# Attention block with a gated feed-forward, one Trainium2 core: start-up loads, a bias transposed on TensorE, and the last tile stored in three parts

## The chip, the cores and the metric

The kernel runs on one NeuronCore of one Trainium2 chip. The metric is device time in microseconds (us) of one execution, the median over several executions. TensorE is called PE here, VectorE DVE, ScalarE ACT, GpSimd POOL and SyncE SP. "PEld" is the weight load of a matmul, which the profile lists apart from the matmul.

## The reference

The block normalises x (2048 rows of 512), feeds the result to attention over a cached K and V (32 heads of 128, 2048 keys) and to a feed-forward layer of width 1792 with squared ReLU, and adds the product of both to x:

```python
def _A_ref(x, k_cache, v_cache, wq, wo):
    q = (x @ wq).reshape(B, Sq, 32, 128).transpose(0, 2, 1, 3)
    scores = jnp.einsum("bhqd,bhkd->bhqk", q, k_cache) * (128 ** -0.5)
    p = _softmax(scores, axis=-1)
    o = jnp.einsum("bhqk,bhkd->bhqd", p, v_cache)
    return o.transpose(0, 2, 1, 3).reshape(B, Sq, 32 * 128) @ wo

def _B_ref(x, w1, b1, w2, b2):
    h = jnp.einsum("bsd,df->bsf", x, w1) + b1
    r = jnp.where(h > 0, h, 0)
    return jnp.einsum("bsf,fd->bsd", r * r, w2) + b2

xn = _layernorm(x)
return x + _A_ref(xn, ...) * _silu(_B_ref(xn, ...))
```

All inputs are bf16.

## The kernel before

**Groups and steps.** The 2048 query rows are cut into four blocks of 512. A group `g` is one head of one block, so there are 128 groups. Each group is cut into eight steps `k`, and each step takes two tiles of 128 keys; the steps of the whole kernel are counted by `pi`, from 0 to 1023. A step issues two score matmuls (128x512, `psA<-qt_sb,kT`), one exponential on ACT over both (`pT<-psA`, 128x1024), and, for the step two back, eight matmuls of the probabilities with V (`psO<-v_sb,pT`, 128x129; column 129 is the sum of the row). The eight PV matmuls go to two PSUM banks of `psO`, two query tiles each. After the last step of a group, DVE copies the two banks out (`o_un<-psO`), takes the reciprocal of the sums and writes the normalised tile `o_bf`; a DMA transposes that to `oT`.

**Fillers.** All other matmuls are cut into single 128x512 matmuls and are put between the scores and the PV matmuls of a step, mostly one or two in each: the query projection of later groups (`job_proj`, `psF<-xnT,wq_sb`), the first feed-forward layer (`job_h`), the second (`job_o2`) and the output projection (`job_wo`). `fill_one` takes them from a list sorted by due time; a credit spreads what is left evenly over the steps. The jobs use the two PSUM banks of `psF` in turn, so that a job's first matmul waits until DVE has emptied the bank used two jobs earlier. Each engine runs its instructions in the order in which they are emitted.

**Order of the PV matmuls.** `gen_pv` goes through a step's matmuls key tile by key tile (n = 0, 1), all four query tiles in each; only the last step of a group (k = 7) goes bank by bank. The first PV step of a group (k = 0) waits for the copies of the group before: its matmuls 1 and 2 need the first bank, matmul 3 the second.

**Start.** The DMAs of the start are emitted in a fixed order. SP issues x tile 0, K of group 0, V of group 0, the query weights `wq` of groups 1 and 2, chunk 0 of `w1` (`load_w1(0)`), K and V of group 1 and chunks 1 to 3 of `w1`. Only then come the refills that belong to a step: `wq` of group `g+3` and K of group `g+2` in step k = 0, V of group `g+2` in step k = 1. ACT issues x tiles 1 to 3 and `wq` of group 0. DVE, POOL and ACT normalise the four x tiles, PE transposes them, and the first query projection is done in four parts (`first_proj`). DVE empties them in two copies (`first_evac`), after which the first scores can start. PE runs matmuls on a tile of zeros (`warm_up`) ahead of that.

**Bias.** `b1` (1792 values) is needed with 128 consecutive values down the partitions, 14 columns. A DMA issued by POOL gathers it in that layout (`_dma_gather`, L217), and DVE casts it to f32 (`b1f`) directly after the two first copies. `job_h` adds it.

**End.** The output projection of the last 16 heads is written out by hand as a tail. The last query tile is done in two halves of 256 columns; each half ends in two DVE operations (`tmp_t`, then `out_t`) and a store from SP.

Of the kernel before, what the change touches and what calls it, by code (L numbers as in the profile page):

```python
# [5 lines left out]
ACT = mybir.ActivationFunctionType  # L6
ALU = mybir.AluOpType
BF16 = mybir.dt.bfloat16
F32 = mybir.dt.float32
P = 128  # L10
# [201 lines left out]
    return e.dma_start(out, in_, transpose=True)  # L212


def _dma_gather(nc, e, out, in_):
    with nc.allow_non_contiguous_dma(reason="tiny one-time bias gather"):
        return e.dma_start(out, in_)  # L217


def bass_recurrent_scan__mha_block_cached__dense_activation_squared_relu__prompt_kernel(  # L220
    nc: bass.Bass,
    A_x: bass.AP,
# [11 lines left out]
    _, Sq, D = A_x.shape  # L234
# [4 lines left out]
    NQB = Sq // QB  # L239
    TPB = QB // P  # L240
# [3 lines left out]
    NFC = F // P  # L244
# [7 lines left out]
    CH = [[(m * HC, (m + 1) * HC) for m in range(NCH)] for _ in range(NQB - 1)]  # L252
# [4 lines left out]
    S = _Sched()  # L257
    PE = S.eng("PE")
    AC = S.eng("ACT")
    DV = S.eng("DVE")  # L260
    GP = S.eng("POOL")
    SP = S.eng("SP")
    E = S.emit

    sb = nc.alloc_sbuf_tensor
# [12 lines left out]
    qt_sb = sb("qt_sb", [P, NQS, QB], BF16)  # L278
# [4 lines left out]
    r_t = sb("r_t", [P, 2, QB], BF16)  # L283
    z_t = sb("z_t", [P, 2, D], F32)
    th_t = sb("th_t", [P, 2, D], BF16)
    b1b = sb("b1b", [P, NFC], BF16)
    b1f = sb("b1f", [P, NFC], F32)
    b2bc = sb("b2bc", [P, D], BF16)
    x_ln = sb("x_ln", [P, TPB, D], BF16)
# [6 lines left out]
    ident = sb("ident", [P, P], BF16)  # L296
# [11 lines left out]
    def bankF(i):  # L308
        return psF[:, i * 512:(i + 1) * 512]
# [8 lines left out]
    sl_b1 = S.slot("b1")  # L318
# [10 lines left out]
    t_ident = E(GP, partial(_ts, out=ident[:], in0=identf[:], scalar1=0.0, scalar2=None,  # L329
                            op0=ALU.is_equal), deps=[t_idf])  # L330
# [11 lines left out]
    def ln_load(j, i, eng=SP):  # L342
        jt = j * TPB + i
        t_xl[jt] = S.emit_dma(
            eng, partial(_dma, out=x_ln[:, i, :], in_=A_x[0, jt * P:(jt + 1) * P, :]), sl_xl[i],
            deps=[t_xn.get(jt - TPB)])
# [60 lines left out]
                  deps=[t_wqfill[0], tok_xT[0][i]], inc=(c == NDC - 1))  # L407
        t_proj[0] = t

    def first_evac(i, n):  # L410
        t_evac[0] = t_bankF[i // 3] = E(
            DV, partial(_copy, out=qt_sb[:, 0, i * P:(i + n) * P],
                        in_=bankF(i // 3)[:, i * P:(i + n) * P]), deps=[t_proj[0]])

    def warm_up(n):
        for _ in range(n):
# [4 lines left out]
    t_kfill = [None] * NG  # L421
# [4 lines left out]
    t_proj = [None] * NG  # L426
    t_evac = [None] * NG
# [3 lines left out]
    t_exp = [None] * NPAIR  # L431
# [36 lines left out]
    def gen_scores(pi):  # L468
        g, k = divmod(pi, NPR)
        s2, i = pi % 2, g % NSL  # L470
        assert t_kfill[g] is not None and t_evac[g] is not None
        t = None
        for n in range(2):
            tt = 2 * k + n
            t = E(PE, partial(_mm, out=psA[:, s2 * 1024 + n * 512:s2 * 1024 + (n + 1) * 512],
                              lhsT=kT[:, i, tt * P:(tt + 1) * P], rhs=qt_sb[:, g % NQS, :],
                              start=True, stop=True),
                  deps=[t_exp[pi - 2] if pi >= 2 else None, t_kfill[g], t_evac[g]],
                  inc=(n == 1))
        if k == NPR - 1:  # L480
            t_S_last[g] = t
        t_exp[pi] = E(AC, partial(_act, out=pT[:, pi % NPT, :],
                                  in_=psA[:, s2 * 1024:(s2 + 1) * 1024],
                                  func=ACT.Exp, scale=SM_SCALE),
                      deps=[t, t_PV[pi - NPT] if pi >= NPT else None])

    def gen_pv(pi):
        g, k = divmod(pi, NPR)
        i = g % NSL
        last = k == NPR - 1  # L490
        order = [(n, qt) for n in range(2) for qt in range(TPB)]
        if last:
            order = [(n, qt) for b in range(2) for qt in (2 * b, 2 * b + 1) for n in range(2)]
        t_bank = [None, None]
        t = None
        for idx, (n, qt) in enumerate(order):
            tt, b = 2 * k + n, qt // 2
            tt_first = tt == 0
            inc = idx == 7 or (last and idx == 3)
            t = E(PE, partial(_mm_shared, out=psO[:, b, qt % 2, 0:Dh + 1],  # L500
                              lhsT=pT[:, pi % NPT, n * QB + qt * P:n * QB + (qt + 1) * P],
                              rhs=v_sb[:, i, tt, 0:Dh + 1],
                              start=(tt_first and qt % 2 == 0), stop=(tt == NKT - 1)),
                  deps=[t_exp[pi], t_vfill[g], t_ones,
                        t_oev[g - 1][b] if g >= 1 else None], inc=inc)
            if inc:
                t_bank[b] = t
        t_PV[pi] = t
        if last:
            t_PV_last[g] = t  # L510
            s = g % 2
            for b in range(2):
                t_oev[g][b] = E(DV, partial(_copy, out=o_un[:, s, 2 * b:2 * b + 2, 0:Dh + 1],
                                            in_=psO[:, b, :, 0:Dh + 1]),
                                deps=[t_bank[b], t_onorm[g - 2] if g >= 2 else None])
            tr = E(DV, partial(_recip, out=rden[:, s, :], in_=o_un[:, s, :, Dh]),
                   deps=[t_oev[g][0], t_oev[g][1], t_onorm[g - 2] if g >= 2 else None])
            base = rden[:, s, :]
            rb = bass.AP(tensor=base.tensor, offset=base.offset,
                         ap=[list(base.ap[0]), [1, TPB], [0, Dh]])  # L520
            t_onorm[g] = E(DV, partial(_tt, out=o_bf[:, s, :, :], in0=o_un[:, s, :, 0:Dh], in1=rb,
                                       op=ALU.mult),
                           deps=[tr, tok_oT[g - 2] if g >= 2 else None])
# [8 lines left out]
    t_bankF = [None, None]  # L532
# [8 lines left out]
    t_rt = [None, None]  # L541
# [13 lines left out]
    def at(step, fn):  # L555
        events.setdefault(step, []).append(fn)

    def job_proj(g):
# [15 lines left out]
            return t_evac[g]  # L574
        return NDC, mm, evac

    def job_h(j, c):
        js = slice(j * QB, (j + 1) * QB)
        box = [None]

        def mm(n, bank):
            box[0] = E(PE, partial(_mm, out=bankF(bank), lhsT=w1_sb[:, n, c * P:(c + 1) * P],
                                   rhs=xnT[:, n, js], start=(n == 0), stop=(n == NDC - 1)),
                       deps=[tok_w1[w1_chunk(c)], t_bankF[bank]] + tok_xT[j], inc=(n == NDC - 1))

        def evac(bank, step):
            s = c % 2
            t1 = E(DV, partial(_ts, out=r_t[:, s, :], in0=bankF(bank), scalar1=b1f[:, c:c + 1],
                               scalar2=0.0, op0=ALU.add, op1=ALU.max),
                   deps=[box[0], t_b1, t_rt[s]])  # L590
            t_h2[j, c] = t_rt[s] = E(
                DV, partial(_tt, out=h2T[:, c, :], in0=r_t[:, s, :], in1=r_t[:, s, :],
                            op=ALU.mult),
                deps=[t1] + [t_o2[j - 1, qt] for qt in range(TPB) if j > 0])
            return t1
        return NDC, mm, evac
# [101 lines left out]
                                op=ALU.add), deps=[t, tok_xt[jt]])  # L698


    jobs = []
    for g in range(1, NG):
        jobs.append((NPR * g - 15, NPR * (g - 2), job_proj(g), g))
    for j in range(NQB):
        b = 30 + j * (SPB - 6)
        for c in range(NFC):
            k = b + (SPB * 9 // 256) * c
            jobs.append((k, max(k - 130, 4), job_h(j, c), None))
        for qt in range(TPB):
            k = b + (SPB * 9 // 256) * NFC + (SPB * 28 // 256) * qt  # L710
# [32 lines left out]

    m, half = len(CH[-1]) - 1, D // 2
    nt = H - CH[-1][-1][0]
    tail = [job_wo(NQB - 1, m, qt) for qt in range(TPB - 1)]
    tail.append(job_wo(NQB - 1, m, TPB - 1, 0, half))
    tail.append(job_wo(NQB - 1, m, TPB - 1, half, D))  # L750
    n_in, n_after = 14, 22
    n2 = n_in + n_after - 2 * (nt - 1)
    tail_order = [(i, x) for i in range(2) for x in range(nt - 1)] + [(2, x) for x in range(n2)]
    tail_order += [(0, nt - 1), (1, nt - 1)] + [(2, x) for x in range(n2, nt)]
    tail_order += [(i, x) for i in range(3, TPB + 1) for x in range(nt)]
    tail_place = {}

    def tail_one(step):
# [20 lines left out]
    def load_w1(i):  # L779
        c0, c1 = [(0, 4), (4, 8), (8, 11), (11, 14)][i]  # L780
        tok_w1[i] = S.emit_dma(
            SP, partial(_dma, out=w1_sb[:, :, c0 * P:c1 * P], in_=w1_view[:, :, c0 * P:c1 * P]),
            sl_w1[i])

    ln_load(0, 0)
    for i in range(1, TPB):
        ln_load(0, i, AC)
    fill_k(0)
    fill_wq(0, AC)
    E(AC, partial(_act, out=th_t[:, 0, 0:1], in_=warm[:, 0:1], func=ACT.Exp), deps=[t_warm])  # L790
# [3 lines left out]
    load_w1(0)  # L794
    fill_k(1)
    fill_v(1)
    for i in range(1, 4):
        load_w1(i)
    for i in range(TPB):
        ln_stats(0, i)  # L800
        if i < 2:
# [14 lines left out]
    first_transpose(3)  # L816
    first_copy(3, DV)
    first_proj(2)
    first_evac(0, 3)
    first_proj(3)  # L820
    first_evac(3, 1)
    tok_b1 = S.emit_dma(GP, partial(_dma_gather, nc, out=b1b[:],
                                    in_=B_b1.rearrange("(c p) -> p c", p=P)), sl_b1)
    tok_b2 = S.emit_dma(GP, partial(_dma, out=b2bc[:],
                                    in_=bass.AP(tensor=B_b2.tensor, offset=B_b2.offset,
                                                ap=[[0, P], [1, D]])), sl_b2)
    t_b1 = E(DV, partial(_copy, out=b1f[:], in_=b1b[:]), deps=[tok_b1])
    tok_w2 = None

    def load_w2():  # L830
# [18 lines left out]
    for pi in range(NPAIR):  # L849
        g, k = divmod(pi, NPR)  # L850
# [76 lines left out]
```

The softmax here doesn't subtract the row's maximum and nothing guards it: scores larger than these inputs give would overflow.

## Time and profile before

| | |
|---|---|
| median of three runs | 1245.47 us (1244.31 to 1246.5) |
| the profiled execution's own time | 1247.03 us |
| its span in the profile | 1245.2 us |
| PE busy | 1226.2 us, 98% |
| ACT busy | 1057.1 us, 85% |
| DVE busy | 471.0 us, 38% |
| mean granted TensorE clock | 0.999 |

The span is the time between the first and the last instruction that the profile shows; 1.8 us of the execution's own time lie outside it. Matmuls are pipelined: a 128x512 matmul is shown as 379 ns, but one starts every 0.216 us, so the starts count and not the durations. Sums of busy time hide where an engine waits; the timeline and the table of waits show that. The four slices of 31 us at the start carry 208 to 220 GB/s of DMA traffic, the middle of the kernel about 145.

### The profile page before, as it was taken

How to read it: one execution, taken by the hardware profiler on the slowest of the kernel's cores; microseconds unless marked ns; L12 is line 12 of the kernel's file. 1: busy time of each engine (PE TensorE's matmuls, PEld its weight loads, DVE VectorE, ACT ScalarE, POOL GpSimd, SP SyncE). 2: the span in 40 equal slices, each digit the busy share in tenths (PEclk: the TensorE clock that was granted, in tenths of full speed). 3: DMA queues.
4: the chain of work that ended last, by engine and by line, in shares of the span. 5: the costliest groups of instructions: out<-in, count | busy, mean ns of one | idle time of the engine just before them, and what ended most of it. 6: DMA issues, size and time to landing. Idle time of an engine off the chain costs nothing.

```text
span 1245.2 us, 26489 instructions
## 1 busy us (share of the span) xinstructions
PE 1226.2 (98%) x11568; PEld 814.4 (65%) x11776; DVE 471.0 (38%) x946; ACT 1057.1 (85%) x1047; POOL 32.9 (3%) x74
## 2 busy tenths in 40 slices
PE   8999999999999999999999999999999999999998
PEld 4666666666666666666666666666666666666665
DVE  3453332344444333333543533233434333324333
ACT  5888888888888888888888888888888888888885
POOL 1001000000001000000000200000000000000000
PEclk9999999999999999999999999999999999999999
DMA  9999977877787888877887998678778878878861
GB/s 220 219 208 216 170 133 132 145 142 139 130 165 154 154 146 140 144 140 131 144 147 152 170 158 141 132 146 142 135 137 147 150 153 153 141 135 144 145 124 31
DMA packets 686835, 185.39 MB, mean 149 GB/s; under 512 B 675168, under 2 KB 685792, under 8 KB 686720
## 3 DMA queue, kind: packets, MB, share of 16 engines
q1 hardware_dynamic: 684320, 179.36, 79.0%
q0 software_dynamic: 1440, 3.81, 1.2%
q8 instruction: 93, 1.52, 0.5%
q10 hardware_dynamic: 960, 0.52, 0.2%
q14 instruction: 22, 0.18, 0.0%
HBM read 96.08 MB, written 2.10 MB: 79 GB/s over the span
## 4 chain that ended last, share of the span: by engine, by line
PE 97%; SPq 1%; issue 1%; DMA 1%; ACT 0%; DVE 0%
PE psO L157 37%; PE psA L152 35%; PE psF L152 24%; SPq L208 1%; DMA wq_sb<-in_A_wq_dram 1%; SPq L212 1%; ACT pT L161 0%; DVE tmp_t L175 0%; DVE out_t L165 0%
## 5 line engine op out<-in xcount | busy, mean ns | idle before, releaser
L161 ACT ACTIVATE pT<-psA 128x1024 bf16<-128x1024 f32 x1024 | 1045.7, 1024 | 168.6 <-PE psA L152 121.3
L157 PEld LDWEIGHTS psO<-v_sb,pT 128*128 128x128 bf16 x8192 | 549.0, 98 | 244.6 <-issue 14.2
L157 PE MATMUL psO<-v_sb,pT 128*128 128x129 bf16 x8192 | 634.6, 220 | 0.5
L152 PE MATMUL psA<-qt_sb,kT 128*128 128x512 bf16 x1853 | 567.3, 379 | 10.9 <-DVE qt_sb L179 0.7
L179 DVE COPY o_un<-psO 128x258 f32<-128x258 f32 x256 | 97.4, 422 | 406.7 <-PE psO L157 405.9
L152 PE MATMUL psF<-xnT,wq_sb 128*128 128x512 bf16 (+1 forms) x516 | 167.0, 376 | 2.5 <-DMA wq_sb<-in_A_wq_dram 2.2
L152 PE MATMUL psF<-wo_all,oT 128*128 128x512 bf16 x479 | 164.1, 379 | 0.1
L152 PEld LDWEIGHTS psA<-qt_sb,kT 128*128 128x128 bf16 x2048 | 158.3, 98 | 1.4 <-issue 0.6
L179 DVE CAST qt_sb<-psF 128x512 bf16<-128x512 f32 (+1 forms) x129 | 88.4, 686 | 99.6 <-PE psF L152 96.0
L152 PEld LDWEIGHTS psF<-xnT,wq_sb 128*128 128x128 bf16 x524 | 50.8, 98 | 63.4 <-DMA wq_sb<-in_A_wq_dram 2.7
L165 DVE TENSOR_TENSOR o_bf<-o_un,rden 128x512 bf16<-128x512 f32 x128 | 88.6, 692 | 4.6 <-DVE rden L183 0.3
L171 DVE TENSOR_SCALAR r_t<-psF,b1f 128x512 bf16<-128x512 f32 x56 | 42.0, 749 | 113.2 <-PE psF L152 111.3
L152 PEld LDWEIGHTS psF<-wo_all,oT 128*128 128x128 bf16 x480 | 46.9, 98 | 56.4
L152 PE MATMUL psF<-xnT,w_sb 128*128 128x512 bf16 x223 | 77.3, 379 | 0.5 <-DVE qt_sb L179 0.5
L152 PE MATMUL psF<-w_sb,h2T 128*128 128x512 bf16 x221 | 73.0, 379 | 0.0
L152 PEld LDWEIGHTS psF<-xnT,w_sb 128*128 128x128 bf16 x224 | 21.9, 98 | 27.2 <-issue 1.0
L152 PEld LDWEIGHTS psF<-w_sb,h2T 128*128 128x128 bf16 x224 | 21.9, 98 | 26.4
L165 DVE TENSOR_TENSOR z_t<-psF,b2bc 128x512 f32<-128x512 f32 x16 | 11.1, 692 | 65.7 <-PE psF L152 55.6
L165 DVE TENSOR_TENSOR acc<-psF,acc 128x512 f32<-128x512 f32 x28 | 19.3, 689 | 35.9 <-PE psF L152 35.9
L208 POOL DMA_DIRECT2D out_dram<-out_t x12 | 6.7, 556 | 885.3 <-DVE out_t L165 885.3
L165 DVE TENSOR_TENSOR h2T<-r_t 128x512 bf16<-128x512 bf16 x56 | 23.8, 425 | 1.9
L183 DVE RECIPROCAL rden<-o_un 128x4 f32<-128x4 f32 x128 | 22.9, 179 | 4.4
(41 smaller groups left out, 152.2 us busy)
## 6 DMA issues: line engine op xcount, KB each, us to landing
v_sb<-in_A_v_cache_dram SPq DMA_DIRECT2D x128, 512.0 KB, 4.8
wq_sb<-in_A_wq_dram SPq DMA_DIRECT2D x127, 128.0 KB, 3.1
wo_all<-in_A_wo_dram SPq DMA_DIRECT2D x4, 1024.0 KB, 6.4
kT<-in_A_k_cache_dram SPq DMA_TRANSPOSE x128, 4.6
oT<-o_bf SPq DMA_TRANSPOSE x128, 3.9
x_t<-in_A_x_dram POOLq DMA_DIRECT2D x16, 128.0 KB, 3.5
w_sb<-in_B_w_dram SPq DMA_DIRECT2D x1, 1792.0 KB, 10.3
x_ln<-in_A_x_dram SPq DMA_DIRECT2D x13, 128.0 KB, 2.8
```

What stands on the lines that cost most here:

```text
L152: return e.matmul(out, lhsT, rhs, start=start, stop=stop)
L157: return e.matmul(out, lhsT, rhs, start=start, stop=stop, skip_group_check=True)
L161: return e.activation(out, in_, func, bias=bias, scale=scale)
L165: return e.tensor_tensor(out, in0, in1, op)
L171: return e.tensor_scalar(out, in0, scalar1=scalar1, scalar2=scalar2, op0=op0, op1=op1)
L179: return e.tensor_copy(out, in_)
L183: return e.reciprocal(out, in_)
L208: return e.dma_start(out, in_)
L212: return e.dma_start(out, in_, transpose=True)
```

## The change

The change has six parts.

1. x tiles 0 and 2 are issued by SP and 1 and 3 by ACT (before: 0 by SP, the others by ACT).
2. Chunk 1 of `w1` is issued in the first group's steps, after `wq` of group 3 and K and V of group 2; chunks 2 and 3 after `wq` of group 4 and K and V of group 3. (The entries stand at steps 0 and 8; what stands there is run from the first step with k of at least 2.)
3. `b1` is loaded as 14 rows of 128 values. A new job at the head of the list transposes the rows on PE into a `psF` bank in step 3, and DVE copies the result to `b1f`.
4. The first copy of the first projection (384 columns) is done by ACT, the second by DVE.
5. The PV matmuls of k = 0 go bank by bank, as those of k = 7 do.
6. The last query tile is done and stored in three parts, of 256, 128 and 128 columns.

The due-time list holds one more job, so the fillers of many steps move by one place; their number is the same but for the new one.

```diff
-    b1b = sb("b1b", [P, NFC], BF16)
+    b1b = sb("b1b", [NFC, P], BF16)
...
-    def first_evac(i, n):
-        t_evac[0] = t_bankF[i // 3] = E(
-            DV, partial(_copy, out=qt_sb[:, 0, i * P:(i + n) * P],
-                        in_=bankF(i // 3)[:, i * P:(i + n) * P]), deps=[t_proj[0]])
+    def first_evac(i, n, eng):
+        out, in_ = qt_sb[:, 0, i * P:(i + n) * P], bankF(i // 3)[:, i * P:(i + n) * P]
+        op = (partial(_act, out=out, in_=in_, func=ACT.Copy) if eng is AC
+              else partial(_copy, out=out, in_=in_))
+        t_bankF[i // 3] = E(eng, op, deps=[t_proj[0]])
...
-                  deps=[t_exp[pi - 2] if pi >= 2 else None, t_kfill[g], t_evac[g]],
+                  deps=[t_exp[pi - 2] if pi >= 2 else None, t_kfill[g], t_evac[g],
+                        t_bankF[0] if pi == 0 else None],
...
-        if last:
+        if last or k == 0:
             order = [(n, qt) for b in range(2) for qt in (2 * b, 2 * b + 1) for n in range(2)]
...
+    def job_b1():
+        box = [None]
+        def mm(n, bank):
+            box[0] = E(PE, partial(_peT, out=bankF(bank)[:, 0:64].bitcast(BF16)[:, 0:NFC],
+                                   in_=b1b[:], ident=ident[0:NFC, 0:NFC]),
+                       deps=[tok_b1, t_ident, t_bankF[bank]])
+        def evac(bank, step):
+            t_b1[0] = E(DV, partial(_copy, out=b1f[:],
+                                    in_=bankF(bank)[:, 0:64].bitcast(BF16)[:, 0:NFC]),
+                        deps=[box[0]])
+            return t_b1[0]
+        return 1, mm, evac
...
-    jobs = []
+    jobs = [(3, 3, job_b1(), None)]
...
+    cuts = [0, D // 2, 3 * D // 4, D]
-    tail.append(job_wo(NQB - 1, m, TPB - 1, 0, half))
-    tail.append(job_wo(NQB - 1, m, TPB - 1, half, D))
+    tail += [job_wo(NQB - 1, m, TPB - 1, c0, c1) for c0, c1 in zip(cuts, cuts[1:])]
...
-    ln_load(0, 0)
-    for i in range(1, TPB):
-        ln_load(0, i, AC)
+    for i in range(TPB):
+        ln_load(0, i, SP if i % 2 == 0 else AC)
...
-    for i in range(1, 4):
-        load_w1(i)
+    at(0, partial(load_w1, 1))
+    at(8, partial(load_w1, 2))
+    at(8, partial(load_w1, 3))
...
-    first_evac(0, 3)
+    first_evac(0, 3, AC)
     first_proj(3)
-    first_evac(3, 1)
-    tok_b1 = S.emit_dma(GP, partial(_dma_gather, nc, out=b1b[:],
-                                    in_=B_b1.rearrange("(c p) -> p c", p=P)), sl_b1)
+    first_evac(3, 1, DV)
+    t_evac[0] = t_bankF[1]
+    tok_b1 = S.emit_dma(GP, partial(_dma, out=b1b[:], in_=B_b1.rearrange("(c p) -> c p", p=P)),
+                        sl_b1)
...
-    t_b1 = E(DV, partial(_copy, out=b1f[:], in_=b1b[:]), deps=[tok_b1])
```

More of the change, by code (lines that the diff above doesn't have):

```diff
@@ L212, in _dmaT @@
     return e.dma_start(out, in_, transpose=True)
-def _dma_gather(nc, e, out, in_):
-    with nc.allow_non_contiguous_dma(reason="tiny one-time bias gather"):
-        return e.dma_start(out, in_)
 def bass_recurrent_scan__mha_block_cached__dense_activation_squared_relu__prompt_kernel(
@@ L575, in job_proj @@
         return NDC, mm, evac
+    t_b1 = [None]
+    def job_b1():
[10 more added lines that the diff above has]
+        return 1, mm, evac
     def job_h(j, c):
@@ L589, in evac @@
                                scalar2=0.0, op0=ALU.add, op1=ALU.max),
-                   deps=[box[0], t_b1, t_rt[s]])
+                   deps=[box[0], t_b1[0], t_rt[s]])
             t_h2[j, c] = t_rt[s] = E(
@@ L742, in fill_one @@
         return True
-    m, half = len(CH[-1]) - 1, D // 2
+    m = len(CH[-1]) - 1
+    cuts = [0, D // 2, 3 * D // 4, D]
     nt = H - CH[-1][-1][0]
     tail = [job_wo(NQB - 1, m, qt) for qt in range(TPB - 1)]
-    tail.append(job_wo(NQB - 1, m, TPB - 1, 0, half))
-    tail.append(job_wo(NQB - 1, m, TPB - 1, half, D))
+    tail += [job_wo(NQB - 1, m, TPB - 1, c0, c1) for c0, c1 in zip(cuts, cuts[1:])]
     n_in, n_after = 14, 22
@@ L754, in bass_recurrent_scan__mha_block_cached__dense_activation_squared_relu__prompt_kernel @@
     tail_order += [(0, nt - 1), (1, nt - 1)] + [(2, x) for x in range(n2, nt)]
-    tail_order += [(i, x) for i in range(3, TPB + 1) for x in range(nt)]
+    tail_order += [(i, x) for i in range(3, len(tail)) for x in range(nt)]
     tail_place = {}
```

## The prediction

> **What bounds the kernel now.** I read the engine shares first, then the waits of PE, then the timeline where those waits lie.
>
> ```profile
> PE 1226.2 (98%) x11568; PEld 814.4 (65%) x11776; DVE 471.0 (38%) x946; ACT 1057.1 (85%) x1047; POOL 32.9 (3%) x74
> ...
> PE 97%; SPq 1%; issue 1%; DMA 1%; ACT 0%; DVE 0%
> ...
> PE psF L152 <- DMA wq_sb<-in_A_wq_dram: 2.2, 1, 2.2
> PE psA L152 <- DVE qt_sb L179: 0.7, 1, 0.7
> PE psF L152 <- DVE qt_sb L179: 0.5, 1, 0.5
> ```
>
> PE is the bound: 97% of the chain. A change pays only where PE stands still, and PE waits in few places, nearly all before 25 us. The timeline shows these.
>
> ```profile
> 15.78 0.59 PE L152 MATMUL psA<-qt_sb,kT 128*128 128x512 bf16 x2
> 16.88 0.59 PE L152 MATMUL psF<-xnT,w_sb 128*128 128x512 bf16 x2 [0.51 <-DVE qt_sb L179]
> ...
> 21.71 0.59 PE L152 MATMUL psA<-qt_sb,kT 128*128 128x512 bf16 x2
> 24.50 0.39 PE L152 MATMUL psF<-xnT,wq_sb 128*128 128x512 bf16 x1 [2.19 <-DMA wq_sb<-in_A_wq_dram]
> ...
> 13.19 4.11 SPq L208 DMA_DIRECT2D w_sb<-in_B_w_dram  x3
> 17.34 0.54 SPq L208 DMA_DIRECT2D wq_sb<-in_A_wq_dram  x1
> ...
> 15.97 0.18 DVE L179 CAST b1f<-b1b 128x14 f32<-128x14 bf16 x1 [4.90 <-DMA b1b<-in_B_b_dram]
> 16.05 1.28 DVE L179 CAST qt_sb<-psF 128x512 bf16<-128x512 f32 x2
> ```
>
> The scores at 21.71 fill PE's slots until 22.14 (two slots of 0.216); the next matmul starts at 24.50, when `wq` of group 3 lands. Its DMA was issued at 17.34, behind three chunks of `w1` (4.11 us of issuing), and took 7.1 us to land. The smaller wait at 16.88 has another root than the named one: DVE stood in front of the `b1` gather until 15.97, so the copies that empty `psF` started at 16.05, though their matmuls were done earlier. A third loss follows the long wait, in the table of stretches:
>
> ```profile
> 24.45:25.60 1.15, 1.10 (x11) 0.76 (x12) 0.00 (x0) 0.00 (x0) 0.00 (x0) 1.00 1.23 277
> 25.60:29.30 3.70, 3.70 (x22) 2.31 (x22) 2.11 (x5) 1.92 (x2) 0.00 (x0) 0.54 1.10 207
> ```
>
> The last three columns are granted clock, DMA share and GB/s. The clock falls to 0.54 for 3.7 us; two 128x512 matmuls there take 0.86 us of the chain instead of 0.43.
>
> A fourth loss is spread over the kernel and stands in no table of waits. At a group's first PV step one sees this:
>
> ```profile
> 1223.69 0.76 DVE L179 COPY o_un<-psO 128x258 f32<-128x258 f32 x2 [6.72 <-PE psO L157]
> ...
> 1224.23 0.61 PEld L157 LDWEIGHTS psO<-v_sb,pT 128*128 128x128 bf16 x8 [0.20 <-issue]
> 1224.36 0.66 PE L157 MATMUL psO<-v_sb,pT 128*128 128x129 bf16 x8
> ```
>
> Eight PV matmuls normally show 0.62 and take 0.45 of the chain; here 0.66 and 0.49. In fine windows the third matmul starts at 1224.51 instead of 1224.475: its weight load starts at 1224.50, just after the second copy ends (1224.45). The timeline has 65 whole blocks with 0.66, and the built program has 66 groups with one filler ahead of the first PV step; with two or three, PE comes late enough.
>
> **What the Trainium skill says.** "TensorE: Matmul & The Clock Gate", Part 1: The HAM clock gate, gives a half-rate clock after an idle window of about 3.4 us and some 3.4 us of work to leave it. The trace agrees on the half rate (0.43 us a matmul against 0.216) and the length (3.7 us), though the visible gap was only 2.36 us. "DMA: Bandwidth & Descriptors", Rules for kernel authors, says that a non-contiguous last dimension makes one descriptor per element, and that several issuing queues save issue time, not bandwidth. Here the 3.5 KB gather took 1.31 us to issue, where the larger `b2` load took 0.57.
>
> **Part 2, `w1` behind the refills.** `wq` of group 3 moves to where the first of the three chunks stood, 13.2 us. With what stands ahead of it unchanged it lands 6.2 to 7.1 us later (V just ahead took 6.2, itself 7.1), at 19.4 to 20.3. PE wants it one step later than before, about 22.4 in the new order. The whole wait goes: 22.14 to 24.50, **2.36 us**, and with it the low clock: 3.7 us at 0.54 loses **1.7 us**. Who is late next? K of group 2 lands earlier than now (26.3). Chunk 1 is issued near 20.6, after V of group 2, and lands by 26 to 28 (7.1 us before); the program wants it in step 20, near 35. Chunks 2 and 3 stand behind V of group 3, which waits for the PV of step 7 (near 22.5), so are issued near 26 and land by 33; their first use is step 38. `wq` of group 4, K and V of group 3 and the first `oT` transpose are moved past at most 1.5 to 4 us of issuing and have a group of slack. No new wait: range of this part 0 to 4.1 us, taken 4.06.
>
> **Part 3, `b1`.** DVE no longer waits; the copies follow their matmuls, and the wait between 16.21 (end of the score slots) and 16.88 goes: 0.67 us. Added are one transpose of 14 columns on PE (the page's floor for small matmuls is 25 ns; at most one slot, 0.22), one DVE copy of 0.18 beside PE's work and a wait on PE: the transposed rows must be there at about 15.9. Issued at about 8.4 to 8.9 in 14 rows of 256 bytes, they may take as long as `b2` (6.3, landing at 14.7 to 15.2) or the old gather (7.1, landing at 16.0). All PE work of step 3 is queued behind that wait, and with it ACT's next exponential. Taken: **0.6 us**; bounds 0.7 and -0.2.
>
> **Parts 1 and 4, the first scores.**
>
> ```profile
> 7.09 0.69 DVE L200 BATCH_NORM_STATS2 st_t<-x_ln 128x6 f32<-128x512 bf16 x1 [0.43 <-DMA x_ln<-in_A_x_dram]
> ```
>
> x tile 3 landed 5.4 us after its issue, behind K's transposes; now it is ACT's second DMA, about 0.5 us earlier, ahead of them. DVE gains the 0.43. PE's transpose of tile 3 waited 0.28 for DVE, and before it come ACT copies that don't move, so only about 0.3 arrives at the first scores. K of group 0 is issued 0.4 later and lands near 8.5, wanted at 11. The 384 columns on ACT (near 0.6, as its 128x512 copies of 0.59) end by about 10.8, together with DVE's last copy. Taken **0.3**; bounds 0.45 and -0.3 (the ACT copy late).
>
> **Part 5, PV bank by bank.** The second bank is now wanted by the fifth matmul's weights, at 1224.53 in the example; it is free for them at 1224.50. So the stall goes in each one-filler group: 66 x 0.04 = **2.6 us**. The new order has 83 such groups and one with none (0.1 at most). The order itself costs nothing: in k = 7 it shows 0.62 too. Bounds: 0 (the weight load is late for another reason) and 2.8.
>
> **Part 6, the tail.**
>
> ```profile
> 1240.97 0.91 DVE L165 TENSOR_TENSOR out_t<-tmp_t,acc 128x256 bf16<-128x256 f32 x1
> 1242.25 0.43 DVE L175 SCALAR_TENSOR_TENSOR tmp_t<-psA,g_all 128x256 f32<-128x256 f32 x1 [0.38 <-PE psA L152]
> 1242.71 0.42 DVE L165 TENSOR_TENSOR out_t<-tmp_t,acc 128x256 bf16<-128x256 f32 x1
> ```
>
> DVE had 0.38 to spare and now gets two more operations. From 0.43 at 256 columns and 0.68 at 512, 128 take about 0.3. The middle part runs from 1241.9 to 1242.5, the last to 1243.15; before, it ended at 1243.13. Its store is smaller (1.6 us to land at 64 KB, 1.7 at 128). Taken 0; bounds 0.3 and -0.3.
>
> **Sum.** 4.06 + 0.6 + 0.3 + 2.6 + 0 = 7.5 us. PE has no slack from 24.5 us to the tail, so what is saved ahead arrives at the end. Against the profiled execution: 1247.03 - 7.5 = 1239.5. Against the median, 1.6 lower, it would be 1237.9; but the runs shown differ by 2.2 us, most likely in these waits and the low clock, which then aren't there to be saved. I take **1239.0 us**.
>
> **Rivals.**
> - *Only the start pays.* The k = 0 stall stays, for the second bank comes only 0.03 us ahead of need: gain 4.9, 1241.6 on the same footing. For it: the narrow slack. Against: every stalled block lost the same 0.04, so the copies are regular.
> - *The low clock stays.* Some other short gap triggers it, as 2.36 us was less than the page's window: gain 5.8, 1240.7. Against: the gaps up to 0.7 us before 22 kept 1.00.
> - *Slower: PE takes over DVE's wait for `b1`.* PE waits in order, so late rows stop everything. A landing at 16.0 costs 0.1. To lose the other 6.9 us and 2.5 more, the rows must land after about 25 us (a stall of 9 us, less the clock loss that it would bring back, 1.7). That gives some 1248. Nothing near shows such a landing; the software queue's worst is 7.1 us.
> - *The change doesn't do what it says.* The DMA engines are saturated in the first 24 us, and `wq` of group 3 may be late wherever it stands: gain 3.4, 1243. Against: 1.3 MB leave the traffic ahead of it.
>
> **How the numbers follow.** My forecast has 0.65, the first two rivals 0.17 together, no saving from the reorder 0.07, a slower kernel 0.04; the rest is a mixture of small misses. About 0.2%, 2.5 us, is what a measurement here can tell from no change: faster ends at 1243.0. Faster 0.88, same 0.08, slower 0.04. The range runs from 1236.6 (all upper bounds, from the median) to 1242.8.
>
> **What would show it.** Right: no wait on `wq` among PE's waits; clock 1.00 in all the first windows; no 0.66 block at k = 0; the DVE copies of `qt_sb` near 14.4 and 15.6; first scores near 10.9; the tail after the last matmul as long as now. Wrong: a PE wait on `b1b` or `w1`, a low-clock stretch anywhere, or PV blocks of 0.66 with the stall at the fifth matmul.

## The result, and the profile after

| | before | changed |
|---|---|---|
| median of six runs | 1246.79 us (1244.31 to 1247.99) | 1240.39 us (1239.98 to 1241.52) |
| profiled execution, and its span | 1247.03, 1245.2 | 1240.14, 1238.3 |

The ratio over all runs is 0.9954, with a 95% interval of 0.9941 to 0.9966 (the quotient of the two medians alone is 0.9949). The kernel is faster by 0.46%, clear of the 0.2%; the forecast of 1239.0 is 1.4 us low. Profile against profile, the execution lost 6.9 us where the sum had 7.5.

The page of the changed kernel, with engine shares and chain:

```profile
PE 1232.8 (100%) x11793; PEld 813.7 (66%) x11793; DVE 472.4 (38%) x947; ACT 1057.3 (85%) x1048; POOL 32.3 (3%) x74
...
PE 98%; DMA 1%; DVE 0%; ACT 0%; issue 0%; POOL 0%; SPq 0%; DVEq 0%
```

The busy time of PE rose to 1232.8 because the profile of before missed 208 of its matmul records (11568 of 11776, where every weight load is there). The matmuls added are 17: the transpose of `b1`, and 16 because the last 256 columns are done in two parts of half the width. The waits of PE (us in total, times, longest), the largest after the wait for the tile of zeros:

```profile
PE psA L152 <- DVE qt_sb L179: 0.4, 1, 0.4
PE psA L196 <- ACT xn_t L161: 0.3, 1, 0.3
PE psF L152 <- DMA wq_sb<-in_A_wq_dram: 0.3, 1, 0.3
```

The timeline of the start, with SP's queue below:

```profile
10.75 1.02 PE L152 MATMUL psA<-qt_sb,kT 128*128 128x512 bf16 x4 [0.43 <-DVE qt_sb L179]
...
15.32 0.59 PE L152 MATMUL psA<-qt_sb,kT 128*128 128x512 bf16 x2
15.85 0.18 PE L196 MATMUL psF<-ident,b1b 14*128 14x14 bf16 x1
15.96 0.39 PE L152 MATMUL psF<-xnT,w_sb 128*128 128x512 bf16 x1
...
21.69 0.59 PE L152 MATMUL psA<-qt_sb,kT 128*128 128x512 bf16 x2
22.12 0.59 PE L152 MATMUL psF<-xnT,wq_sb 128*128 128x512 bf16 x2
...
14.26 3.04 SPq L208 DMA_DIRECT2D wq_sb<-in_A_wq_dram  x1
```

The transpose of `b1` takes the place of one filler (in step 4, not 3 as I wrote: the second projection still had two matmuls left in step 3). The projection of group 3 follows its scores without a gap: its `wq` was issued at 14.26 and landed 7.6 us later, at 21.82, just before its weight load at 21.91. Granted clock, after the busy times and counts, stays at 1.00:

```profile
24.00:36.00 12.00, 12.00 (x120) 7.99 (x118) 5.75 (x11) 10.47 (x11) 0.00 (x0) 1.00 1.10 246
```

A group's first PV step with one filler ahead of it:

```profile
22.98 0.76 DVE L179 COPY o_un<-psO 128x258 f32<-128x258 f32 x2 [0.33 <-PE psO L157]
23.52 0.57 PEld L157 LDWEIGHTS psO<-v_sb,pT 128*128 128x128 bf16 x8 [0.20 <-issue]
23.65 0.62 PE L157 MATMUL psO<-v_sb,pT 128*128 128x129 bf16 x8
```

The first weight load is as late as before, but the eight matmuls take 0.62, as everywhere else. No whole block of 0.66 is left; the one group with no filler ahead shows 0.64.

And one wait that I did not forecast, on `wq` of group 6:

```profile
49.83 0.39 PE L152 MATMUL psF<-xnT,wq_sb 128*128 128x512 bf16 x1 [0.29 <-DMA wq_sb<-in_A_wq_dram]
```

To see where the time went, I took the start of each step's second score weight load and subtracted the matmuls issued before it (0.216 us for each of 512 columns, 0.0568 for each PV matmul). What remains is PE's delay. A matmul takes slightly less than these figures, so this measure sinks by some 2 us over a kernel where nothing waits; only the differences between the two kernels count. Changed kernel against before, in these two profiles:

| at step | before | changed | gained so far | what lies between |
|---|---|---|---|---|
| 4 | 11.41 | 10.95 | 0.46 | first scores (parts 1 and 4) |
| 5 | 12.08 | 11.17 | 0.91 | `b1`, 0.45, its own slot paid (part 3) |
| 12 | 16.09 | 11.15 | 4.94 | `wq` wait and low clock, 4.03 (part 2) |
| 34 | 16.09 | 11.57 | 4.52 | the new wait, -0.42 |
| 1008 | 16.60 | 9.55 | 7.05 | spread over all groups, 2.53 (part 5) |
| 1023 | 16.65 | 9.66 | 6.99 | the last groups |

From the modelled end of the last matmul to the end of the span it is 2.98 us before and 3.05 after (part 6: nothing gained, 0.07 lost).

### The profile page after: what moved, and what is told of

Same layout as the page of the kernel before. It is cut to its first block, busy times and chain, and to the rows that moved or that the text cites. A ratio compares the mean times of both kernels' runs of the same rounds, so it can differ in the third digit from the quotient of the medians.

```text
span 1238.3 us, 26720 instructions
## 1 busy us (share of the span) xinstructions
PE 1232.8 (100%) x11793; PEld 813.7 (66%) x11793; DVE 472.4 (38%) x947; ACT 1057.3 (85%) x1048; POOL 32.3 (3%) x74
## 4 chain that ended last, share of the span: by engine, by line
PE 98%; DMA 1%; DVE 0%; ACT 0%; issue 0%; POOL 0%; SPq 0%; DVEq 0%
PE psO L157 37%; PE psA L152 36%; PE psF L152 25%; DMA wq_sb<-in_A_wq_dram 1%; DMA x_ln<-in_A_x_dram 0%; DVE out_t L165 0%; DVE tmp_t L175 0%; PE psA L196 0%; ACT xn_t L161 0%; DVE o_un L179 0%; DVE st_t L200 0%; DVE o_bf L165 0%; ACT xnT L161 0%; POOL rstd L165 0%; DVE qt_sb L179 0%
## 5 line engine op out<-in xcount | busy, mean ns | idle before, releaser
L152 PE MATMUL psA<-qt_sb,kT 128*128 128x512 bf16 x2048 | 609.0, 379 | 0.5 <-DVE qt_sb L179 0.4
```

What stands on the lines that cost most here:

```text
L152: return e.matmul(out, lhsT, rhs, start=start, stop=stop)
```

## The experiments

Ratios are over all runs, against the kernel before on the same chip, whose median was 1246.26 us beside E1 to E4, 1246.79 beside E5 to E8 and 1246.46 beside E9 to E12. "Delay" is PE's delay as in the table above. Each execution has its mean granted TensorE clock on record, as a share of full speed: in the kernel before it is 1.000 in 42 of these 78 executions (median 1245.88 us) and 0.997 to 0.999 in the other 36 (median 1247.74). The profiled execution of before, with its low clock of 3.7 us, is one with 0.999.

**E1, part 5 alone.**

```diff
-        if last:
+        if last or k == 0:
```

> The kernel before with part 5 alone: the PV matmuls of k = 0 go bank by bank. If the third matmul stood for the copy of the second bank, 66 groups lose 0.04 us less: no PV block of 0.66 is left and the span falls by 2.6 us, with the wait on wq near 22 us and the low clock after it unchanged. If the stall only moves to the fifth matmul, or another cause delays the weight load, the blocks of 0.66 stay and the time is the same.

Measured: 1244.93 us, 0.9985 [0.9978, 0.9991]; every whole PV block at 0.62, and a gain in delay that grows evenly from step 13 to step 1023 by 2.65 us. For the PV blocks the first account holds. The median gains only 1.3 us. One difference is on record: the granted clock is below 1.000 in 15 of 21 executions here and in 13 of 30 of the kernel before. Among executions at 1.000 the medians differ by 2.1 us, among those at 0.999 by 2.4. Why the low clock comes more often is not shown.

The start of the profiled execution was not that of before, as the expectation had it: its first scores came at 14.01 instead of 11.21, because x tile 3, on ACT's queue, landed late (DVE waited 2.85 us for it). Before them PE stood 1.59 us for the `wq` of the prologue, with shorter gaps behind, and the clock was at 0.50 from 12 to 18 us, so this start also cost more than the one of before. The wait on `wq` of group 3, 2.19 us in before, was only 0.56 here.

**E9, the same stall removed by cover instead of order.**

```diff
-            if not (credit >= 1.0 or late):
+            if not (credit >= 1.0 or late or (k == 2 and n < 2)):
```

> The kernel before, its PV order unchanged, but with at least two fillers in each step k = 2, so that PE comes 0.22 us later to the first PV matmuls of the 66 groups that had one. If these stand only because the copy of the second bank ends 0.05 us too late, the blocks of 0.66 vanish without any change of the order, and the part of the gain that grows over the kernel is 2.6 us here too. If the order of the matmuls itself costs, the blocks stay at 0.66 and nothing is gained.

Measured: 1245.32 us, 0.9988 [0.9981, 0.9995]; no block of 0.66 and an evenly growing gain of 2.6 us in the trace, with the order of before. So the order has no price of its own; the stall was the second bank's copy, seen only where PE came early. The median gains 1.1 us, and again more executions are below 1.000: 18 of 20, against 11 of 24 of the kernel before. At like clock the medians differ by 1.9 us (1.000, only two executions here) and 2.7 (0.999).

**E2, part 2 alone.**

```diff
-    for i in range(1, 4):
-        load_w1(i)
+    at(0, partial(load_w1, 1))
+    at(8, partial(load_w1, 2))
+    at(8, partial(load_w1, 3))
```

> The kernel before with part 2 alone: chunks 1 to 3 of w1 behind the refills. If the order of the queue made wq of group 3 late, the wait of 2.36 us goes and with it the low clock of 1.7 us: 4.1 us less, clock 1.00 in all windows; PE waits on wq of group 6 near 54 us or a little, if at all, for the load of w2 stands ahead of it in both. If the DMA engines are the limit whatever the order, wq still lands near 24 us, half of the wait stays, and the low clock with it: under 2 us less.

Measured: 1243.72 us, 0.9980 [0.9971, 0.9989]. PE has no wait on `wq` after the first scores, and the clock is 1.00 throughout. In this execution the first scores came at 12.70, 1.5 us later than in the profile of before; from there to step 20 PE gained 4.13 us on it. The mechanism is right, but the median gains only 2.5. Not every execution of before had 4 us to lose: its granted clock is 1.000 in 17 of 30 executions (in 8 of 10 here), and where the start was late, the wait on `wq` of group 3 was shorter: 0.56 in E1 and 0.65 in E3, both with `w1` in its old place. At 1.000 on both sides the medians differ by 2.3, about the wait without the low clock.

**E8, part 2 undone in the changed kernel.** The diff of E2, reversed.

> The changed kernel with part 2 undone: chunks 1 to 3 of w1 stand ahead of wq of group 3 again. If this order made the wait, wq lands near 25.5 us, PE waits some 3.5 us for it and runs at the low clock for 3.7 us after it: 4 to 5.5 us more than the changed kernel, near 1245. If most of the gain in the start came from elsewhere, it is less than 2 us more.

Measured: 1244.30 us, 0.9979 [0.9968, 0.9990], about 4 us above the changed kernel, but from 1241.74 to 1246.53. The profiled execution was one of the short ones:

```profile
24.18 0.61 PE L152 MATMUL psF<-xnT,wq_sb 128*128 128x512 bf16 x2 [1.71 <-DMA wq_sb<-in_A_wq_dram]
```

The wait of 1.71 us left the clock at 1.00. So the median agrees with my 4.06 while this one trace, with 1.9 us of added delay, does not. The granted clocks tell the two kinds apart: 1.000 in the four executions up to 1243.23, and 0.997 to 0.999 in the five from 1244.30 on.

**E3, part 3 alone.** `b1` as rows, `job_b1`, and the two waits that follow from it, as in the change.

> The kernel before with part 3 alone: b1 as rows, transposed on PE. The wait of 0.67 us ahead of the first job_h goes and one slot of 0.22 us for the transpose is added, so PE is 0.45 us earlier at 22 us. If the wait on wq is set by the landing of its DMA, that wait grows by the same 0.45 us and the span stays at that of before. If what is saved ahead is kept, the span falls by 0.45 us.

One execution: 1246.38 us. Inconclusive on the main question, because its first scores came at 13.34, 2.1 us later than in the profile of before, and the waits on `wq` behind them cannot be compared. PE's delay rose by 0.21 from step 4 to step 5 instead of 0.67, the 0.45 that I counted. Without part 5 the added job also costs something: it shifts the fillers, and the trace has 83 PV blocks of 0.65 or 0.66, 17 more than the 66, which at 0.04 each is 0.7 us.

**E4 and E5, parts 1 and 4 alone.**

```diff
-    ln_load(0, 0)
-    for i in range(1, TPB):
-        ln_load(0, i, AC)
+    for i in range(TPB):
+        ln_load(0, i, SP if i % 2 == 0 else AC)
...
-    first_evac(0, 3)
+    first_evac(0, 3, AC)
```

> The kernel before with parts 1 and 4 alone: x tiles over both queues, the first copy on ACT. The first scores start 0.46 us earlier (10.75 instead of 11.21). SP issues one DMA more ahead of K of group 0, and in the changed kernel its stream ran 1.1 us late by V of group 1. If that delay is due to this part, wq of group 3 lands about 1 us later than before, near 25.5, the wait on it grows from 2.4 to about 4 us, and the span is up to 1 us longer. If it is due to something else, the wait grows by 0.46 alone and the span is unchanged.

The one execution took 1252.07 us, and neither account fits:

```profile
23.40 0.17 DVE L179 CAST b1f<-b1b 128x14 f32<-128x14 bf16 x1 [12.76 <-DMA b1b<-in_B_b_dram]
24.31 1.01 PE L152 MATMUL psF<-xnT,w_sb 128*128 128x512 bf16 x2 [8.41 <-DVE qt_sb L179]
```

The first scores came at 10.74, as expected. But the gather of `b1` landed 15.2 us after its issue; DVE stood in front of it, PE behind DVE, and the clock was at 0.50 from 21 to 27 us.

> Parts 1 and 4 alone once more, now timed. In the single look the old b1 gather landed 15.2 us after its issue (7.1 in the kernel before) and PE stood for 8.4 us. If the earlier start brings the gather into this every time, the median is near 1252, some 5 us above the kernel before. If that execution was a stray one, the median is within 1 us of the kernel before and most executions have no long wait for qt_sb.

Measured: 1249.24 us (1248.37 to 1253.13), 1.0029 [1.0015, 1.0042]. Parts 1 and 4 alone make the kernel slower. The profiled execution shows how an earlier start is lost, and more:

```profile
16.95 0.17 DVE L179 CAST b1f<-b1b 128x14 f32<-128x14 bf16 x1 [6.08 <-DMA b1b<-in_B_b_dram]
17.86 0.59 PE L152 MATMUL psF<-xnT,w_sb 128*128 128x512 bf16 x2 [1.73 <-DVE qt_sb L179]
26.43 0.39 PE L152 MATMUL psF<-xnT,wq_sb 128*128 128x512 bf16 x1 [3.14 <-DMA wq_sb<-in_A_wq_dram]
```

Here `b1` took 8.7 us. `wq` of group 3 was issued at 19.24, where it was 17.34 before, and the low clock followed the wait of 3.14.

**E6, part 3 undone in the changed kernel.** `_dma_gather` and the cast on DVE are back, and `job_b1` is not in the list.

> The changed kernel with part 3 undone: b1 gathered again, cast by DVE. If the gather lands about 7 us after its issue, near 15.3, DVE holds the copies until then, and the time is within 0.5 us of the changed kernel. If the late landing belongs to the early start (parts 1 and 4), b1 comes near 23.4, PE stands for about 8 us and the low clock adds 1 to 2: 1248 to 1251, slower than the kernel before. The rows of part 3 are then what carries the change, not the 0.45 us that I counted for them.

Measured: 1244.42 us, from 1240.49 to 1252.0; 0.9987 [0.9970, 1.0004]. In the profiled execution, one of the shorter ones at 1242.01, the gather took 8.3 us, PE waited 1.49 for the copies behind it, and 0.82 for `wq` of group 7 near 61.5 us. Without part 3 the change is not clearly faster than before. The rows are worth about 4 us in the median, not 0.45, and most of the spread goes with them. The granted clock is below 1.000 in eight of these twelve executions and in none of the six of the changed kernel; what the longest two met, at 1252, was not profiled.

**E10, the gather beside the rows, with nobody waiting for it.**

```diff
+    S.emit_dma(GP, spare, sl_b1g)    # b1 gathered into a tile that nobody reads
```

> The changed kernel with the old gather of b1 issued besides, after b1 and b2, into a tile that nobody reads. If the gather hurt only because DVE waited for its landing, the time is that of the changed kernel within 0.5 us. If its 1792 two-byte elements hold up the other transfers, wq, K or V of the first groups land late, PE waits for one of them, and the median is 2 us or more above the changed kernel, with a wide spread.

Measured: 1239.95 us (1239.73 to 1240.46), 0.9940 [0.9924, 0.9956]: the time of the changed kernel. The spare gather, issued after `b1` and `b2`, took 7.9 us to land. So it is DVE's wait in its queue that hurts, and not the gather's traffic. The wait on `wq` of group 6 was 0.64 us in this execution, against 0.29 in the changed kernel.

**E11, part 1 undone in the changed kernel.**

```diff
-        ln_load(0, i, SP if i % 2 == 0 else AC)
+        ln_load(0, i, SP if i == 0 else AC)
```

> The changed kernel with part 1 undone: x tiles 1 to 3 on ACT. If x tile 3 behind the transposes of K is what made the first scores late (11.2 in one execution of the kernel before, 12.7 to 14.0 in three looks at kernels with that order), they start at 11 to 14 us instead of 10.8 and the time is 1 to 3 us above the changed kernel. If the 0.3 us of my sum is typical, the time is within 0.5 us of it.

Measured: 1240.91 us, 0.9945 [0.9929, 0.9962], not to be told from the changed kernel by time. In the trace x tile 3 came late and the first scores with it:

```profile
8.19 0.69 DVE L200 BATCH_NORM_STATS2 st_t<-x_ln 128x6 f32<-128x512 bf16 x1 [1.50 <-DMA x_ln<-in_A_x_dram]
12.26 1.02 PE L152 MATMUL psA<-qt_sb,kT 128*128 128x512 bf16 x4 [0.43 <-DVE qt_sb L179]
```

That is 1.5 us of delay, of which 0.45 is given back near 50 us, where the wait on `wq` of group 6 is gone. PE that is later meets that load when it has landed.

**E12, the changed kernel again.**

> The changed kernel as it is, on the same chip as the three others, to compare them with: 1240 to 1241.5 us.

Measured: 1240.07 us in the median, 0.9944 [0.9925, 0.9963], but one of five executions took 1244.41, and it is the profiled one:

```profile
52.40 0.39 PE L152 MATMUL psF<-xnT,wq_sb 128*128 128x512 bf16 x1 [2.89 <-DMA wq_sb<-in_A_wq_dram]
...
48.00:60.00 12.00, 9.11 (x70) 5.64 (x69) 3.50 (x7) 6.29 (x7) 0.00 (x0) 0.86 0.86 172
```

The wait of 0.29 grew to 2.89, and the low clock came with it; delay rose by 4.7 us in all. SP's queue, first here and then in the changed kernel's own profile, shows why:

```profile
37.92 1.59 SPq L208 DMA_DIRECT2D w_sb<-in_B_w_dram  x1
39.55 5.80 SPq L212 DMA_TRANSPOSE oT<-o_bf  x1
45.40 0.58 SPq L208 DMA_DIRECT2D wq_sb<-in_A_wq_dram  x1
...
37.87 2.21 SPq L208 DMA_DIRECT2D w_sb<-in_B_w_dram  x1
40.12 3.32 SPq L212 DMA_TRANSPOSE oT<-o_bf  x1
43.49 1.11 SPq L208 DMA_DIRECT2D wq_sb<-in_A_wq_dram  x1
```

The 1792 KB of `w2` go out first; the transpose behind them takes 5.80 us to issue instead of 3.32, and `wq` waits behind that: it is issued 1.9 us later and takes 7.0 us to land instead of 6.3. Why this transpose took longer stays open.

**E7, a version that answers it:** the changed kernel with `w2` in four parts, one per group, and `wq` of group 3 ahead of K of group 1.

```diff
-    at(2 * NPR, load_w2)
+    for i, (c0, c1) in enumerate([(0, 4), (4, 8), (8, 11), (11, NFC)]):
+        at((2 + i) * NPR, partial(load_w2, c0, c1))
...
+    fill_wq(3)
     fill_k(1)
```

> The changed kernel with two edits: w2 loaded in four parts, one per group from group 2 on, and wq of group 3 issued ahead of K of group 1. If the wait of 0.45 us near 49.8 (wq of group 6) comes from the 1792 KB of w2 ahead of it in the queue, it goes; and wq of group 3, which landed at 21.85 for a need at 21.9, gets several us of margin. PE has no wait after the first scores and the span is 0.45 us under that of the changed kernel, 1237.8, with less spread. If w2 is not the cause, the wait on wq stays near 50 us and the time is the same.

Measured: 1239.80 us, from 1239.70 to 1240.18, 0.9948 [0.9935, 0.9960]. No wait on `wq` is left, and from step 32 to step 34 it keeps the 0.45 that the changed kernel loses. SP's queue, with 512 KB of `w2` in it instead of 1792:

```profile
37.41 2.22 SPq L208 DMA_DIRECT2D w_sb<-in_B_w_dram  x1
39.68 1.21 SPq L212 DMA_TRANSPOSE oT<-o_bf  x1
40.93 0.58 SPq L208 DMA_DIRECT2D wq_sb<-in_A_wq_dram  x1
```

`wq` of group 6 lands 4.2 us after its issue. In the median this version is level with the changed kernel within what these runs can tell. Five executions without a long one do not show that the occasional 1244 is gone, since the changed kernel had one in eleven; what is shown is that the wait behind it is gone in this trace.

## Why the prediction was right, step by step

- **Part 2: right.** 4.06 forecast, 4.03 in the pair of profiles; the wait and the low clock went together. It is the price of an execution with the low clock, though, and fewer than half of those of before were that. The idle window of about 3.4 us that the Trainium skill states ("TensorE: Matmul & The Clock Gate", Part 1: The HAM clock gate) is too long for what these runs show: the clock fell after visible gaps of 2.19, 2.89 and 3.14 us and stayed after 1.49, 1.71 and 1.73 (E6, E8, E5), once PE was working steadily; in E1's prologue, where PE has gaps in a row, one of 1.59 went ahead of a low clock. So these gaps give no single threshold. That `wq` would land by 20.3 was wrong: it was 21.82, 0.09 before its weight load, for the DMA took 7.6 us and was issued 1.1 us later than I put it.
- **"No new wait": the step that failed.** I compared each moved load with its need and did not ask which unmoved loads PE would now meet earlier. PE reached the projection of group 6 about 5 us sooner, `wq` of group 6 still stood behind `w2`, and 0.45 us was lost again, 0.8 in E10, 4.7 in E12, and nothing in E11, where PE came later. E7 shows the cause as far as one trace can. Its two edits were not run apart, but the move of `wq` of group 3 hardly reaches this load: `wq` of group 5 is issued at 33.32 there and at 33.66 in the changed kernel, and only behind `w2` does the lead grow to 2.6 us (40.93 against 43.49).
- **Part 3: the right sign, the wrong size.** In the pair of profiles it is 0.45 against 0.6, the wait of 0.67 less the slot of 0.22 for the transpose. The copies of `qt_sb` came at 13.32 and 15.07, earlier than my 14.4 and 15.6. My term came from one landing of 7.1 us. Where x came early (E4, E5, E6) the gather landed after 15.2, 8.7 and 8.3 us; the rows took 3.3 to 6.8 in seven profiled executions. E6 puts the part at about 4 us once the other waits are gone. Why the gather is slower there stays open.
- **Parts 1 and 4: a term of 0.3** that was 0.46 in the pair and 1.5 in E11. The profile of before happened to have x tile 3 at 7.1 us; in E1, E2, E3 and E11 it came at 8.2 to 9.5. That they would slow the kernel when alone (E5) I did not see.
- **Part 5: right.** 2.6 forecast, 2.53, 2.65 and 2.6 in three pairs of profiles, by two different edits. The medians of E1 and E9 show about half of it, and 1.9 to 2.7 us at like clock.
- **Part 6: right at nothing.** DVE's four operations on the last two parts take 0.29 us each, the last store's data are ready 0.15 us later after the last matmul, and its smaller store gives half of that back (1.48 us to land instead of 1.56).
- **The sum: near, in part by luck.** Its terms add up to 7.56; the upper bounds make 8.35, so the lower end of the range, from the median of 1245.47, would be 1237.1, not 1236.6. The parts do not simply add. Alone, the medians moved by -1.3 (part 5), -2.5 (part 2), +2.4 (parts 1 and 4) and nothing in one execution (part 3), little more than 1 us saved in all, where the change saves 6.4. Left out of the changed kernel, part 2 costs about 4 us and so does part 3. Each term was read from one execution of before, in which no trace could show that the earlier start of parts 1 and 4 pays only together with the rows of part 3.
- **The rivals.** "Only the start pays" fell with E1 and E9. "The low clock stays" did not come in the six executions of the changed kernel, all at 1.000, but came in one of five in E12, by the new wait. "`wq` of group 3 is late wherever it stands" missed by 0.09 us: the load came 1.5 us or more later than I had put it. The slower case, PE taking over DVE's wait for late `b1` data, did not come; the late landing exists, but with the gather (15.2 us in E4), not with the rows.

## What to carry to other kernels

Ask of a change that makes the bound engine earlier not only what it moves, but what everything else was timed for: here a 1.8 MB load that the change did not touch stood ahead of the next wait. A wait on a DMA that stands in an in-order engine's queue ties everything behind it to the DMA's slowest landing, so take a transfer's price from several executions, and put a load whose landing varies where nobody queues behind it. A stall of 0.04 us that no table of waits lists is worth 2.6 us when 66 groups pay it; compare the durations of equal blocks to find it.

## What the hardware showed that I had not expected

The start of the same order of DMAs varies by microseconds from one execution to the next: the first scores came at 11.2 to 14.0 us in the six profiled executions with three x tiles on ACT's queue (before, E1, E2, E3, E9, E11), and at 10.7 to 11.0 in the eight with x on both. And SP's queue is held by the issue itself: a DMA transpose of K took 2.7 to 6.3 us to issue in the start of before, so a later load's time is set by what SP still has to issue, before any byte of it moves.
